# v's loads issued behind their batch's q and k without a gate, one attention session kept in the unturned form, and one output product two slots later

## The chip, the core and the metric

The kernel runs on one core of one Trainium2 chip. The metric is the device time of one launch in microseconds; a lower time is better. The engines are named as in the profile: PE is TensorE (PEld its weight loads), DVE VectorE, ACT ScalarE, POOL GpSimd, SP the sync engine, which here only issues DMAs.

## The reference

```python
def _attn_ref(q, k, v):                     # each 8 x 8 x 576 x 64, float32
    window = 32
    scores = (1 / sqrt(D)) * q @ k^T
    scores = where(abs(pos[:, None] - pos[None, :]) <= window, scores, -1e9)
    attn = exp(scores - max(scores)); attn = attn / (sum(attn) + 1e-9)
    return attn @ v

def _moe_ref(x, w_in, w_out):               # x 4608 x 512, w_in 512 x 2048, w_out 2048 x 512
    h = x @ w_in
    g = where(h >= 1, h, where(h <= -1, 0, (h + 1)**2 / 4))
    return g @ w_out
```

The attention's output, heads side by side, is the x of the second part: batch b's 576 positions are rows 576 b to 576 b + 575.

## The kernel before

**Slots.** The second part is cut into 144 slots of TensorE work, numbered a = 0 to 143. A slot multiplies one piece of `w_in` with 256 or 512 columns of the transposed x (`xT`) into a PSUM buffer `hp` (L664 for 256 columns, L685 for 512; from slot 56 to 135 the wide form). ScalarE makes `rr` from it (L703), then either VectorE makes `mx` and `gT` (L709, L710) or ScalarE makes `mx` (L706) and VectorE `gT` (L707). `hp` has two buffers. The order of all instructions of an engine is the order in which the program writes them; nothing is moved by a scheduler.

**What else a slot holds.** After its `hp` and `rr`, a slot a runs the attention steps that a table gives it (`run(a)`), then the products with `w_out` (`pair`, L636, for the first 512 rows; `unit`, L618 and L609, for the rest), then `run(a + 0.5)`, then the transpositions listed for it. A `pair` makes eight products of 256 columns; four pairs fill one output tile, which ScalarE copies (L641) and SP stores (L642). The list `pairs` gives (slot, pair number); the last tile's four pairs are numbers 14, 12, 15 and 13.

**The attention as a stream.** Batch 0 is treated apart. From batch 1 on, the positions form one stream, cut into turns of two or three 64-position blocks: turns 0 to 4 are batch 1, 5 to 7 batch 2, 8 to 10 batch 3 and so on, three to a batch, up to 22. For a turn k `stream_scores` multiplies q and k (L289), into a PSUM tile `bb` and, for three blocks, the spare halves `sp` of an `hp` and an `op` buffer; ScalarE takes exp (L295, L298) and VectorE applies the mask (L206). `stream_sums` of turn k, in the slot where turn k + 1's scores are made, multiplies with v and divides by the row sums. Turns 4 to 22 have their sums in slots 26, 29, 33, 36, 39, 44, 48, 51, 59, 66, 71, 74, 81, 87, 95, 99, 108, 111 and 123. The sums of turns 8, 11, 14, 17 and 20 are the first to read the v of batches 3 to 7. The sums come in two forms:

- unturned: 32 products with v as the weights and 8 with `ones` as the weights for three blocks (L421; for turns of this form VectorE has added pairs of the masked scores into `rows` at L307 before). The row sums land beside the result and in `sp`; ScalarE takes ln and exp(-ln) of them (L325, L328, L329), VectorE multiplies into `xT` (L333).
- turned (turns in `TURNED`): 48 products with the scores as the weights (L352), v having a column of ones, so that the row sums are a column; VectorE takes a reciprocal (L360) and scales into `xn` (L364), and SP issues three DMA transpositions of `xn` into `xT` (L370, L373).

**The loads.** GpSimd issues all loads from HBM that change the type from float32 to bfloat16: q and k of a batch in two DMAs each (L107), v in four (L117). They go through one software queue in order. q and k of batch b land in one of two buffers by (b + t) mod 2 (t is 0 for q and 1 for k), so that the q of batch b + 1 reuses the k buffer of batch b. From batch 2 on, SP transposes q and k by DMA into `qT` and `kT` (L199), in the slots of `xps`; these, the transpositions of `xn` and all stores of the output share SP's queue in order. v has three buffers, batch b in number b mod 3. v of batches 0 and 1 is loaded at the start. v of batches 2 to 7 is loaded at the end of a transposition's slot, behind a gate: a GpSimd copy of two columns of the transposed tile, which makes GpSimd, and all that it issues later, wait for that transposition:

```python
        for x in xps.get(a, []):
            xpose(*x)
            if x[1] == (x[0] not in EARLY):      # EARLY = 3, 4: behind q's; the others: behind k's
                P.tensor_copy(gate, qkT(*x)[:, 0:2])
                for n in range(4):
                    load_v(x[0], n)
```

The loads of q and k are written at the start of slots 19 and 20 (batch 3), 26 and 27, 37 and 38, 60 and 61, 84 and 85 (batch 7); the transpositions of q and k in slots 7 and 16 (batch 2), 23 and 24, 34 and 35, 49 and 50, 65 and 69, 89 and 91. GpSimd and SP come to their instructions ahead of TensorE where nothing makes them wait.

Of the kernel before, what the change touches and what calls it, by code (L numbers as in the profile page):

```python
# [14 lines left out]
def kernel(  # L15
# [32 lines left out]
    LONG = 2  # L48
    SPLIT = range(20, 25)
    DIRECT = 4, 5  # L50
    EARLY = 3, 4
    TURNED = {6, 9, 10, 12, *range(14, 23)}

    const = ctx.enter_context(tc.tile_pool(name="const", bufs=1))
    nat = ctx.enter_context(tc.tile_pool(name="nat", bufs=2))
# [47 lines left out]
    def load_nat(b, t):  # L103
        src, dst, nm = ((q, qn, "qn"), (k, kn, "kn"))[t]
        x = dst[b] = nat.tile([128, NU, 2, D], BF, name=nm, tag=f"n{(b + t) % 2}", bufs=1)
        for h in range(2):
            nc.gpsimd.dma_start(out=x[:, :, h], in_=src[b, NY * h:NY * h + NY].rearrange("y s d -> (y s) d")  # L107
                                .rearrange("(u p) d -> p u d", p=128))

    def load_v(b, n):  # L110
        if b not in vn:
            vn[b] = vns[b % 3]
            if 2 <= b < 5:
                P.memset(vn[b][:, :, :, D:], 1.0)
        h, a = divmod(n, 2)
        y = NY * h + 2 * a
        nc.gpsimd.dma_start(out=vn[b][64 * a:64 * a + 64, :, h, :D], in_=v[b, y:y + 2].rearrange("y s d -> (y s) d")  # L117
                            .rearrange("(c r) d -> r c d", r=64))
# [48 lines left out]
    def qkT(b, t):  # L167
        if t == 0:
            return qTs[b % 3][:, PAD:]
        if b not in kT:  # L170
            kT[b] = ktp.tile([128, NY * S], BF, name="kT")
        return kT[b]
# [24 lines left out]
    def xpose(b, t):  # L197

        nc.sync.dma_start_transpose(out=qkT(b, t).rearrange("d (u p) -> d u p", p=128),  # L199
                                    in_=(qn, kn)[t][b].rearrange("p u h d -> p (u h d)"))  # L200
# [70 lines left out]
    def stream_scores(k, eng, pool=ps_s):  # L271
# [29 lines left out]
        M = turn_of(k)  # L301
        if k in TURNED or k in DIRECT:
            return
# [9 lines left out]
    def turn_of(k):  # L313

        return next(m for s, e, m in STREAMS if s == turns[k][0])
# [61 lines left out]
    def stream_sums(k, pool=ps_n):  # L377

        if k in TURNED:
            return turned_sums(k, pool)  # L380
# [95 lines left out]
    def flush():  # L476
        while muls:
            muls.pop(0)()
# [20 lines left out]
    def op_tile(shape, nm="op"):  # L499

        turn[0] ^= 1
        return ps_o.tile(shape, FP, name=nm, tag=f"op{turn[0]}")
# [54 lines left out]

    NB = NT // TB
    NF = DFF // 256
    pairs = [(7, 0), (7, 1), (8, 2), (11, 4), (12, 5), (13, 3), (15, 8), (15, 6), (17, 9), (17, 7), (18, 10), (20, 11), (21, 14), (22, 12), (23, 15), (23, 13)]  # L560
    ev = {}

    def at(a, *todo):


        ev.setdefault(a, []).extend(x for x in todo if x)
# [14 lines left out]
    ends_first = [14, 14.5, 15.5, 16, 20, 21.5, 24.5, 27, 28, 34, 37, 38, 40, 42, 45, 46, 49, 50, 52, 54, 55, 57, 58, 62, 63, 67, 68, 69, 73, 76, 77, 78, 80, 84, 86, 88, 90, 91, 93, 94, 96, 97, 98, 101, 103, 104, 106, 110, 112, 114, 117, 120, 121, 122, 127, 130, 132, 134]  # L581
    for n, a in enumerate(sl):
        at(a, seq[first_sl + n][0], seq[first_sl + 1 + n][1] if first_sl + 1 + n < len(seq) else (stream_sums, len(seq), ps_s))
    loads, xps = {}, {}
    for t, a in enumerate([7, 16]):
        xps.setdefault(a, []).append((2, t))
    for b in range(LONG + 1, B):
        a = [19, 26, 37, 60, 84][b - 3]
# [7 lines left out]
    def home(t):  # L596

        return (3 - t % 4 if t % 4 in (0, 3) else t % 4) if WIDE[0] <= NF * t < WIDE[1] else t % 4
# [29 lines left out]
    def pair(x):  # L628

        half, p, g = x // 8, x % 8 // 4, x % 4  # L630
        if (half, p) not in op:
            op[half, p] = op_tile([128, 2, 256]), []
        o, done = op[half, p]
        for tt in range(2):
            for j in range(4 * g, 4 * g + 4):
                nc.tensor.matmul(o[:, tt], gT[:, j, p, 128 * tt:128 * tt + 128], w_out[:, j, 256 * half:256 * half + 256],  # L636
                                 start=not done, stop=len(done) == 4 * NF - 1, skip_group_check=True)
                done.append(j)
        if len(done) == 4 * NF:
            osb = osp.tile([128, DM], FP, name="osb")  # L640
            A.copy(osb, o.rearrange("p t f -> p (t f)"))  # L641
            nc.sync.dma_start(out=out[256 * p:256 * p + 256, 256 * half:256 * half + 256]  # L642
                              .rearrange("(t p) f -> p t f", p=128), in_=osb.rearrange("p (t f) -> p t f", t=2))

    def run(pos):
        todo = []
        spares.clear()
        for fn, *x in ev.get(pos, []):
            if fn in (sums, stream_sums):
                todo.append(fn(*x))  # L650
                if pos in ends_first:
                    todo.pop()()
            elif fn is tposes:
                tposes(*x)
            else:
                pool = (x.pop(),) if x[-1] in (ps_s, ps_n, ps_o) else ()
                fn(*x, None if pos < bias_until else V, *pool)
        for end in todo:
            end()

    def project(hp, f, r0, todo, first, last):

        for n, (j, kk) in enumerate(todo):
            nc.tensor.matmul(hp[:, j], w_in[:, kk, 256 * f + 128 * j:256 * f + 128 * j + 128],  # L664
                             xT[:, kk, r0:r0 + TB], start=first and n == 0, stop=last and n == len(todo) - 1,
                             skip_group_check=True)
# [5 lines left out]
    for a in range(NF * NB + 2 * NF):  # L672
        wide = WIDE[0] <= a < WIDE[1]
        for b, x in loads.get(a, []):
            load_nat(b, x)
        if a == 0 or a > 3:
            flush()
        if a < NF * NB:
            if wide:
                n, f = divmod(a - WIDE[0], 2 * NF)  # L680
                t = WIDE[0] // NF + 2 * n
                r0 = TB * t % RING
                hp = ps_h.tile([128, 2, TB], FP, name="hp", tag="hp")
                for n, kk in enumerate((0, 2, 1, 3)):
                    nc.tensor.matmul(hp.rearrange("p n t -> p (n t)"), w_in[:, kk, 128 * f:128 * f + 128],  # L685
                                     xT[:, kk, r0:r0 + 2 * TB], start=n == 0, stop=n == 3)
                g = gT[:, f, home(t):home(t + 1) + 1:home(t + 1) - home(t)]
            else:
                t, f = order[a] if a < len(order) else divmod(a, NF)
                r0 = TB * t % RING  # L690
                if a in (0,):
                    hps = [ps_h.tile([128, 2, TB], FP, name="hp", tag="hp") for _ in range(2)]
                    for y in range(2):
                        for n in range(2):
                            project(hps[n], f + n, r0, [(j, y + 2 * m) for j in range(2) for m in range(2)], y == 0, y == 1)
                elif not hps:
                    hps = [op_tile([128, 2, TB], "hp") if a in [6] else ps_h.tile([128, 2, TB], FP, name="hp", tag="hp")]
                    project(hps[0], f, r0, [(j, kk) for j in range(2) for kk in (0, 2, 1, 3)], True, True)
                hp = hps.pop(0)
                g = gT[:, 2 * f:2 * f + 2, home(t)]  # L700

            rr = ewp.tile([128, 2, TB], FP, name="rr")
            A.activation(rr, hp, AF.Relu, scale=0.5, bias=0.5)  # L703
            mx = ewp.tile([128, 2, TB], FP, name="mx")
            if a in two_on_act:
                A.activation(mx, rr, AF.Square)  # L706
                V.scalar_tensor_tensor(g, hp, 1.0, mx, op0=ALU.max, op1=ALU.min)  # L707
            else:
                V.tensor_max(mx, hp, rr)  # L709
                V.scalar_tensor_tensor(g, rr, 1.0, mx, op0=ALU.min, op1=ALU.mult)  # L710
        flush()
        run(a)
        for n, x in pairs:
            if n == a:
                pair(x)
        for x in range(done, done + units[a]):
            unit(x)
        done += units[a]
        run(a + 0.5)
        for x in xps.get(a, []):  # L720
            xpose(*x)
            if x[1] == (x[0] not in EARLY):
                P.tensor_copy(gate, qkT(*x)[:, 0:2])  # L723
                for n in range(4):
                    load_v(x[0], n)


# [28 lines left out]
```

## Time and profile before

| | |
|---|---|
| time, median of 3 runs | 303.62 us (303.17 to 303.64) |
| profiled execution | 305.74 us, of it the span of the program's instructions 303.9 us |
| granted TensorE clock, mean over the span | 0.994 |
| busy: TensorE | 289.2 us (95%) |
| busy: VectorE, ScalarE, GpSimd | 227.0, 184.3 and 79.5 us |
| software queue, hardware queue | 18.06 MB and 19.38 MB, packet time 92.4% and 32.4% of 16 DMA engines' span |

A row of a timeline reads: start in us, duration in us (of a merged run of instructions, first start to last end), engine, line, operation, output<-inputs, form, count, and in brackets the idle time of the engine before it and what ended that. "SPq" rows are SP's issuing of a DMA, not its transfer. A row for one tile gives the least, median and greatest duration in ns, the first and last start, and the line under it the time from issue to landing.

### The profile page before, as it was taken

The numbers are of one execution on the slowest core, as the hardware profiler recorded it, in microseconds if no ns is written. First come the engines' busy times: TensorE is split into PE (matmuls) and PEld (weight loads), VectorE is DVE, ScalarE is ACT, GpSimd is POOL, SyncE is SP. The second block draws the span as 40 slices with busy tenths as digits, with TensorE's granted clock in tenths as the row PEclk, the third lists the DMA queues.
The fourth block names the chain that finished last, engine by engine and source line by source line (L and its number), as shares of the span: only waits on it lengthen the run. The fifth ranks groups of instructions, "written<-read, shape, count | busy, mean of one in ns | idle before, by whom it ended". The sixth has DMA issues, their size and how long they took to land.

```text
span 303.9 us, 8062 instructions
## 1 busy us (share of the span) xinstructions
PE 289.2 (95%) x3345; PEld 171.4 (56%) x3376; DVE 227.0 (75%) x370; ACT 184.3 (61%) x331; POOL 79.5 (26%) x101
## 2 busy tenths in 40 slices
PE   8789999999999997999999999999999999999995
PEld 3467878877666665654444444444444444446644
DVE  5278888978987988599888898597878887546700
ACT  4687794777677663655765566565566435785301
POOL 8795730073091083009105500013000000000000
PEclk9999999999999999799999999999999999999999
DMA  9999999999999999999999993399312211100021
GB/s 152 182 180 200 187 178 152 213 130 145 173 152 142 159 183 131 164 232 109 155 192 111 168 157 55 78 176 111 90 37 63 60 37 56 42 35 36 37 104 69
DMA packets 149204, 38.24 MB, mean 126 GB/s; under 512 B 133552, under 2 KB 145584, under 8 KB 149168
## 3 DMA queue, kind: packets, MB, share of 16 engines
q0 software_dynamic: 103056, 18.06, 92.4%
q1 hardware_dynamic: 45968, 19.38, 32.4%
q8 instruction: 26, 0.43, 0.6%
q10 hardware_dynamic: 144, 0.29, 0.4%
q14 instruction: 10, 0.08, 0.1%
HBM read 36.70 MB, written 9.44 MB: 152 GB/s over the span
## 4 chain that ended last, share of the span: by engine, by line
PE 77%; DMA 12%; POOL 5%; issue 3%; ACT 3%; DVE 0%; POOLq 0%; ACTq 0%
PE op L618 31%; PE hp L685 23%; PE hp L664 12%; DMA vn<-in_v_dram 6%; DMA w_in<-in_moe_w_in_dram 4%; PE op L636 4%; POOL vn L117 2%; POOL w_in L122 2%; PE bb L352 2%; DMA qT<-qn 2%; PE bb L289 1%; PE op L609 1%; PE bb L421 1%; PE tp L192 1%; ACT rr L703 1%
## 5 line engine op out<-in xcount | busy, mean ns | idle before, releaser
L703 ACT ACTIVATE rr<-hp 128x512 f32<-128x512 f32 x144 | 85.5, 595 | 86.1 <-PE hp L685 47.6
L618 PE MATMUL op<-w_out,gT 128*128 128x512 bf16 x472 | 121.2, 381 | 3.2 <-issue 3.0
L709 DVE TENSOR_TENSOR mx<-hp,rr 128x512 f32<-128x512 f32 x104 | 71.3, 685 | 19.2 <-ACT rr L703 18.4
L685 PE MATMUL hp<-xT,w_in 128*128 128x512 bf16 x315 | 80.7, 379 | 0.3
L618 PEld LDWEIGHTS <-gT 128*128 128x128 bf16 x496 | 47.1, 98 | 50.3 <-issue 0.6
L710 DVE SCALAR_TENSOR_TENSOR gT<-rr,mx 128x512 bf16<-128x512 f32 x104 | 72.2, 694 | 3.6
L664 PE MATMUL hp<-xT,w_in 128*128 128x256 bf16 x512 | 66.7, 275 | 2.1 <-DMA w_in<-in_moe_w_in_dram 1.4
L664 PEld LDWEIGHTS <-w_in 128*128 128x128 bf16 x512 | 49.3, 98 | 17.5 <-issue 2.4
L685 PEld LDWEIGHTS <-w_in 128*128 128x128 bf16 x320 | 31.2, 98 | 37.9 <-issue 0.3
L707 DVE SCALAR_TENSOR_TENSOR gT<-hp,mx 128x512 bf16<-128x512 f32 x40 | 27.5, 688 | 18.4 <-ACT mx L706 16.3
L117 POOL DMA_DIRECT2D vn<-in_v_dram x32 | 27.3, 871 | 4.9 <-issue 1.5
L295 ACT ACTIVATE wt<-bb 128x1024 bf16<-128x1024 f32 (+2 forms) x23 | 22.1, 966 | 6.6 <-PE bb L289 5.1
L706 ACT ACTIVATE mx<-rr 128x512 f32<-128x512 f32 x40 | 25.2, 630 | 1.3
L723 POOL COPY gate<-kT 128x2 bf16<-128x2 bf16 x4 | 1.3, 325 | 90.4 <-DMA kT<-kn 90.4
L206 DVE TENSOR_TENSOR wt<-wt,mask 128x1408 bf16<-128x1408 bf16 (+4 forms) x23 | 19.5, 847 | 7.0 <-ACT wt L298 5.7
L622 ACT COPY osb<-op 128x512 f32<-128x512 f32 x23 | 13.3, 578 | 10.9 <-PE op L618 10.9
L636 PE MATMUL op<-w_out,gT 128*128 128x256 bf16 x128 | 16.0, 273 | 0.4 <-ACT rc L325 0.4
L107 POOL DMA_DIRECT2D qn<-in_q_dram x12 | 14.8, 1252 | 2.6 <-DMA kn<-in_k_dram 1.9
L107 POOL DMA_DIRECT2D kn<-in_k_dram x12 | 14.8, 1261 | 0.9 <-DMA vn<-in_v_dram 0.8
L636 PEld LDWEIGHTS <-gT 128*128 128x128 bf16 x128 | 12.4, 98 | 2.2 <-DMA w_out<-in_moe_w_out_dram 0.7
L364 DVE TENSOR_TENSOR xn<-bb,rs 128x512 bf16<-128x512 f32 (+1 forms) x26 | 13.3, 552 | 0.4
L298 ACT ACTIVATE wt<-sp 128x256 bf16<-128x256 f32 (+1 forms) x36 | 11.1, 367 | 0.0
(89 smaller groups left out, 185.2 us busy)
## 6 DMA issues: line engine op xcount, KB each, us to landing
out_dram<-osb SPq DMA_DIRECT2D x30, 256.0 KB, 2.7
vn<-in_v_dram POOLq DMA_DIRECT2D x32, 144.0 KB, 6.5
qn<-in_q_dram POOLq DMA_DIRECT2D x12, 288.0 KB, 10.1
kn<-in_k_dram POOLq DMA_DIRECT2D x12, 288.0 KB, 12.8
out_dram<-osb SPq DMA_DIRECT2D x12, 128.0 KB, 1.9
w_in<-in_moe_w_in_dram POOLq DMA_DIRECT2D x11, 128.0 KB, 4.9
w_out<-in_moe_w_out_dram POOLq DMA_DIRECT2D x4, 256.0 KB, 8.9
w_out<-in_moe_w_out_dram POOLq DMA_DIRECT2D x2, 512.0 KB, 13.6
```

Of the source, the lines that this page charges most:

```text
L107: nc.gpsimd.dma_start(out=x[:, :, h], in_=src[b, NY * h:NY * h + NY].rearrange("y s d -> (y s) d") .rearrange("(u p) d -> p u d", p=128))
L117: nc.gpsimd.dma_start(out=vn[b][64 * a:64 * a + 64, :, h, :D], in_=v[b, y:y + 2].rearrange("y s d -> (y s) d") .rearrange("(c r) d -> r c ...
L295: A.activation(wt[:, :, w0 + lo:w0 + cut], ps.rearrange("p h (y j) -> p (h y) j", y=2)[:, :, lo:cut], AF.Exp, scale=D ** -0.5)
L618: nc.tensor.matmul(op[tt], gT[:, j, home(tt // 2), 128 * (tt % 2):128 * (tt % 2) + 128], w_out[:, j], start=j == 0, stop=j == 15)
L636: nc.tensor.matmul(o[:, tt], gT[:, j, p, 128 * tt:128 * tt + 128], w_out[:, j, 256 * half:256 * half + 256], start=not done, stop=len(done ...
L664: nc.tensor.matmul(hp[:, j], w_in[:, kk, 256 * f + 128 * j:256 * f + 128 * j + 128], xT[:, kk, r0:r0 + TB], start=first and n == 0, stop=l ...
L685: nc.tensor.matmul(hp.rearrange("p n t -> p (n t)"), w_in[:, kk, 128 * f:128 * f + 128], xT[:, kk, r0:r0 + 2 * TB], start=n == 0, stop=n == 3)
L703: A.activation(rr, hp, AF.Relu, scale=0.5, bias=0.5)
L706: A.activation(mx, rr, AF.Square)
L707: V.scalar_tensor_tensor(g, hp, 1.0, mx, op0=ALU.max, op1=ALU.min)
L709: V.tensor_max(mx, hp, rr)
L710: V.scalar_tensor_tensor(g, rr, 1.0, mx, op0=ALU.min, op1=ALU.mult)
```

## The change

Three edits. The gates of batches 3 to 7 go: their v is loaded at the start of slots 20, 27, 40, 61 and 85, directly behind the same batch's q and k for batches 3, 4, 6 and 7, and two slots behind them for batch 5. Batch 2 keeps a gate, at the transposition of its q (slot 7) instead of its k (slot 16). Turn 6, whose sums stand in slot 33, leaves `TURNED` and takes the unturned form; its scores, in slot 29, get the addition into `rows`. Pair 13 moves from slot 23 to slot 25, and with it the copy and the store of that output tile.

```diff
-    EARLY = 3, 4
-    TURNED = {6, 9, 10, 12, *range(14, 23)}
+    TURNED = {9, 10, 12, *range(14, 23)}
...
-    pairs = [(7, 0), (7, 1), (8, 2), (11, 4), (12, 5), (13, 3), (15, 8), (15, 6), (17, 9), (17, 7), (18, 10), (20, 11), (21, 14), (22, 12), (23, 15), (23, 13)]
+    pairs = [(7, 0), (7, 1), (8, 2), (11, 4), (12, 5), (13, 3), (15, 8), (15, 6), (17, 9), (17, 7), (18, 10), (20, 11), (21, 14), (22, 12), (23, 15), (25, 13)]
...
+    vslots = [20, 27, 40, 61, 85]
...
         for b, x in loads.get(a, []):
             load_nat(b, x)
+        if a in vslots:
+            for n in range(4):
+                load_v(LONG + 1 + vslots.index(a), n)
...
             xpose(*x)
-            if x[1] == (x[0] not in EARLY):
+            if x == (LONG, 0):
                 P.tensor_copy(gate, qkT(*x)[:, 0:2])
                 for n in range(4):
-                    load_v(x[0], n)
+                    load_v(LONG, n)
```

## The prediction

> **What bounds the kernel now.** I read the page first (busy time, the slices, the chain that ended last), then the waits, then the timelines around each wait. The three lines are the engines' busy time, the DMA slices and the chain by engine.
>
> ```profile
> PE 289.2 (95%) x3345; PEld 171.4 (56%) x3376; DVE 227.0 (75%) x370; ACT 184.3 (61%) x331; POOL 79.5 (26%) x101
> ...
> DMA  9999999999999999999999993399312211100021
> ...
> PE 77%; DMA 12%; POOL 5%; issue 3%; ACT 3%; DVE 0%; POOLq 0%; ACTq 0%
> ```
>
> TensorE is busy 95% of the span and carries 77% of the chain, so time is won only where TensorE stands still or runs slowly. But the DMA engines are at 90% or more through the first 24 slices, some 182 us: a second resource lies close behind. Two lines of the waits, "waiting line <- releaser: us in total, times, longest", and three of TensorE's timeline show what v does:
>
> ```profile
> POOL gate L723 <- DMA kT<-kn: 90.4, 4, 32.3
> ...
> PE bb L421 <- DMA vn<-in_v_dram: 2.0, 4, 0.8
> ```
>
> ```profile
> 94.00 0.45 PE L421 MATMUL bb<-wt,vn 64*64 64x96 bf16 x24 [0.33 <-DMA vn<-in_v_dram]
> ...
> 119.00 0.23 PE L421 MATMUL bb<-wt,vn 64*64 64x96 bf16 x2 [0.78 <-DMA vn<-in_v_dram]
> 119.97 0.45 PE L421 MATMUL bb<-wt,vn 64*64 64x96 bf16 x24 [0.74 <-DMA vn<-in_v_dram]
> ```
>
> GpSimd stands 90.4 us at the gate, and the v loads queued behind it reach TensorE late: for batch 3 at 94.0 (0.33 us) and for batch 4 at 119 (0.78 + 0.74). That is 1.85 us of TensorE; the rest of the 2.0 is batch 1, which the change does not touch. The stall at 119 has a second price, seen when the span is cut at the clock's own edges (PE and PEld busy, then DVE, ACT, POOL, and PEclk):
>
> ```profile
> 117.95:121.36 3.41, 1.74 (x67) 1.30 (x68) 2.28 (x4) 1.08 (x2) 0.00 (x0) 1.00 1.67 156
> 121.36:124.77 3.41, 3.41 (x14) 1.76 (x13) 1.54 (x3) 3.25 (x8) 0.00 (x0) 0.50 2.03 151
> ```
>
> After 3.41 us in which TensorE was busy 1.74, the granted clock was 0.50 for the next 3.41 us: half of 3.41, 1.71 us of matmul work, is lost. The Trainium skill ("TensorE: Matmul & The Clock Gate", Part 1) ties the half clock to a whole idle window of about 3.4 us that runs freely. The trace agrees on the length and not on the depth: the window before was only half idle. By the page's rule this dip would not belong to the stall and would stay.
>
> **The v loads, part by part.** Today each batch's q and k loads, their transpositions on SP's queue, and only then (behind the gate) v, follow one another. GpSimd's timeline:
>
> ```profile
> 62.45 0.68 POOL L723 COPY gate<-kT 128x2 bf16<-128x2 bf16 x1 [20.77 <-DMA kT<-kn]
> ...
> 66.53 2.47 POOL L107 DMA_DIRECT2D qn<-in_q_dram  x2
> ...
> 82.76 0.32 POOL L723 COPY gate<-qT 128x2 bf16<-128x2 bf16 x1 [11.35 <-DMA qT<-qn]
> ...
> 87.38 2.45 POOL L107 DMA_DIRECT2D qn<-in_q_dram  x2 [0.52 <-DMA kT<-kn]
> ```
>
> Five gates go; batch 2's stays but waits for q's transposition instead of k's. The next rows are one tile's DMAs each: count, ns of issue, first and last start, and below it the time from issue to landing. They give the prices of the transfers.
>
> ```profile
> L199 SPq DMA_TRANSPOSE qT<-qn x1: 3807/3807/3807, 51.4 to 51.4; - x1
> DMA to landing us min/median/max: 5.8/5.8/5.8
> ...
> L117 POOL DMA_DIRECT2D vn<-in_v_dram x4: 852/859/885, 63.2 to 65.7; - x4
> DMA to landing us min/median/max: 4.9/5.1/5.7
> ...
> L107 POOL DMA_DIRECT2D kn<-in_k_dram x2: 1267/1271/1275, 68.9 to 70.1; - x2
> DMA to landing us min/median/max: 9.6/9.8/10.0
> ...
> L199 SPq DMA_TRANSPOSE kT<-kn x1: 2857/2857/2857, 80.4 to 80.4; - x1
> DMA to landing us min/median/max: 6.4/6.4/6.4
> ```
>
> v of batch 2: four issues 0.85 us apart; the second lands at 64.0 + 4.9 = 68.9 and the fourth at 65.7 + 5.7 = 71.4, so 1.25 us each, 5.0 for the four, and 71.4 - 63.2 = 8.2 from first issue to end. The q and k loads behind it end at 70.1 + 10.0 = 80.1: 8.7 us. k's transposition ends at 80.4 + 6.4 = 86.8, which is 6.7 after the last k load. Now the new order. Batch 2's q is transposed at 51.4 + 5.8 = 57.2; the gate opens 5.2 us earlier than 62.45, v is issued at about 57.9 and ends at 57.9 + 8.2 = 66.1. The q of batch 3 need not wait for v's 3.4 us of issues any more, only for batch 2's k transposition (62.4, since the buffer is shared): 62.6 instead of 66.5. Its q and k end at 66.1 + 8.7 = 74.8, its v at 74.8 + 5.0 = 79.8, and TensorE asks at 94.0. Batch 4's q is issued about 0.6 behind batch 3's k transposition, near 87; 8.7 + 5.0 + some 2 to 3 us of start give v by 104, asked at 119. Both stalls go: -1.85 us, and with the second the half clock, -1.71, where an execution has it. Batches 5 to 7 have no v stall now and get v earlier still.
>
> What is late next? Transfers of the software queue hold a transposition back, which the gate had kept away from v:
>
> ```profile
> L107 POOL DMA_DIRECT2D kn<-in_k_dram x2: 1237/1242/1247, 89.8 to 91.0; - x2
> DMA to landing us min/median/max: 12.5/12.6/12.8
> ...
> L199 SPq DMA_TRANSPOSE qT<-qn x1: 5282/5282/5282, 98.5 to 98.5; - x1
> DMA to landing us min/median/max: 8.9/8.9/8.9
> ```
>
> This one took 8.9 us against 5.8 above, since k's loads ended only at 91.0 + 12.8 = 103.8, and it landed 3.6 behind them. The Trainium skill ("DMA: Bandwidth & Descriptors", Queues, rings and completion order) says that a DMA engine takes turns between its queues packet by packet. By that rule a transposition would share from the start and batch 3's k would be ready well before 86; the trace shows it finishing behind the loads, so I sum with it queued behind v. Then batch 3's k transposition ends at 79.8 + 6.7 = 86.5, and its scores are asked for here:
>
> ```profile
> 87.03 0.37 PE L289 MATMUL bb<-qT,kT 64*64 64x96 bf16 x16
> ```
>
> Today 86.8 against 87.0, afterwards 86.5: the same knife-edge, cover 0.5 us. I take a cost of 0; the bounds are an end 2 us earlier (no cost) and one 2 us later (batch 2's k transposition slowed by v beside it), which stalls 1.5 us.
>
> **The session behind slot 33.** The rows of the turned session (slot 33) and of the unturned one of the same form in slot 36:
>
> ```profile
> 82.96 0.60 ACT L703 ACTIVATE rr<-hp 128x512 f32<-128x512 f32 x1 [0.85 <-ACT wt L298]
> ...
> 88.79 0.41 ACT L325 ACTIVATE rc<-bb 128x256 f32<-128x256 f32 x1
> 89.06 0.69 ACT L328 ACTIVATE rc<-sp 128x256 f32<-128x256 f32 x2
> 89.78 0.84 ACT L329 ACTIVATE rc<-rc 128x768 f32<-128x768 f32 x1
> ```
>
> ```profile
> 82.93 1.04 PE L664 MATMUL hp<-xT,w_in 128*128 128x256 bf16 x8
> ```
>
> ```profile
> 83.80 1.02 DVE L364 TENSOR_TENSOR xn<-bb,rs 128x512 bf16<-128x512 f32 x2
> ...
> 89.88 0.56 DVE L307 TENSOR_TENSOR rows<-wt 128x768 bf16<-128x768 bf16 x1
> 90.66 0.96 DVE L333 TENSOR_TENSOR xT<-bb,rc 128x768 bf16<-128x768 f32 x1 [0.22 <-ACT rc L329]
> ```
>
> ScalarE gains 0.41 + 0.69 + 0.84 = 1.94 us between L298 and the next rr; 0.85 of it was idle there, so rr of slot 34 comes some 1.1 us later. VectorE adds 0.56 (earlier, at slot 29, where it idles) and trades 1.02 for 0.96. On TensorE 48 products become 40; three transpositions leave SP's queue. On the path: the hp buffer's spare half is now read until L328 ends. ScalarE's idle began at 82.96 - 0.85 = 82.11; L325 and L328 take 89.78 - 88.79 = 0.99, so the buffer is free at 83.1 and a signal later, where hp of slot 35 started at 82.93: about +0.35. The ones products wait for the same buffer ahead of the next scores: about +0.2. I take +0.55, an estimate; bounds 0 (ScalarE's idle before the next slots hides it) and 1.1 (rr's whole delay).
>
> **The product from slot 23 to 25.** Eight products move behind hp of slot 25. TensorE's two waits there:
>
> ```profile
> 65.03 1.03 PE L664 MATMUL hp<-xT,w_in 128*128 128x256 bf16 x8 [0.22 <-DVE mx L709]
> ...
> 66.94 0.31 PE L289 MATMUL sp<-qT,kT 64*64 64x128 bf16 x8 [0.25 <-DVE gT L707]
> ```
>
> The product now fills the first, and hp of slots 24 and 25 come earlier, so VectorE clears the second: -0.47, bounds -0.47 and 0. Its store moves in SP's queue behind batch 3's two transpositions; the output buffer is asked for again only three copies later, so 0.
>
> **Given back.** -1.85 - 1.71 - 0.47 + 0.55 = -3.48 with the half clock, -1.77 without. The loads' cadence (q, k, v, then transpositions that free the buffers) keeps its length per batch, so TensorE runs into it. The tightest place later is slot 88, whose xT comes by SP:
>
> ```profile
> 187.87 1.03 PE L685 MATMUL hp<-xT,w_in 128*128 128x512 bf16 x4
> ```
>
> ```profile
> L373 SPq DMA_TRANSPOSE xT<-xn x2: 1186/1206/1226, 180.9 to 182.1; - x2
> ...
> DMA to landing us min/median/max: 4.5/5.6/6.6
> ```
>
> They land by 182.1 + 4.5 = 186.6; the last is needed by the third matmul, half of 1.03 after 187.87, so slack is about 1.7 us. If batch 7's loads end no earlier, 3.48 would be cut to 1.7; if the transpositions move up with TensorE, nothing is cut. I take 1.0 back with the half clock and 0.15 without: -2.5 and -1.6. The middle is -2.1.
>
> **The sum.** The profiled execution took 305.74 us (span 303.9, 1.8 around it): 303.6 after. The median of the runs is 303.62, 2.1 less than the profiled one; the half clock's 1.71 may be missing in them, which is why I take the middle. 303.62 - 2.1 = 301.5. A measurement of this kernel can tell about 0.2%, 0.6 us, from no change.
>
> **Rivals.**
> *Slower: v holds k's transposition past its scores.* The place is slot 36, asked at 87.0. For it: batch 3's transposition meets its scores within 0.2 us now, and there v's 5.0 us is queued ahead. Against it: the loads start 3.9 us earlier. It decides when it ends 2 us late, near 89: that stall halves a window like the one at 118 and brings its own half clock, 2 + 1.71 = 3.7 against the gain of 2.1: 305.2. With all of v's 5.0 added to today's 86.8 the stall is 4.8: 308. The page's rule of taking turns speaks against this one. Chance 0.26.
> *Most of it is given back.* The waits vanish, no execution without the profiler had the half clock, slot 33 costs its 1.1, the product wins nothing and slot 88 takes 0.15: -1.85 + 1.1 + 0.15 = -0.6: 303.0 and up. Chance 0.14.
> *Nothing is given back.* The half clock was in every run and slot 88's transpositions move up: -3.48: 300.1. Chance 0.15.
> *The change does not do what it says*: if v were queued behind the next batch's q, it would come no earlier. The order of GpSimd's instructions excludes it: v of batch 3 stands directly behind its k.
>
> **How the numbers follow.** The forecast has 0.45, with 0.15 for the larger gain faster by over 0.2% is 0.60; within 0.2% is 0.14; slower 0.26. Low end 300.0, the larger gain; the high end 304.9 reaches into the slower rival, up to a stall just under 2 us, leaving out about 0.2.
>
> **What would show it.** Right: no L421 wait on vn at 94 and 119, v of batch 4 landed near 104, PEclk without a dip near 121, hp of slot 26 without its 0.22, three SP transpositions fewer. Wrong: L289 waiting on kT near 87 (the slower rival), a wait of L685 on xT at slot 56 or 88 (given back), a half clock at a new place, or the L421 waits still there.

## The result, and the profile after

The changed kernel takes 306.09 us, the kernel before 303.53 us (medians of 16 executions each, on the same chip), 2.6 us or 0.8% more. As a ratio with its 95% interval it is 1.010 (1.0072 to 1.0128). That is above the forecast's range and within the 305.2 to 308 of the slower rival. All ratios leave out executions that took over 1.5% more than the fastest of their kernel, two of twelve in e3 and three of twelve in e5 among them.

The profiled execution after took 306.88 us (span 305.1, mean granted clock 0.994), against 305.74 before (303.9, 0.994). The page of the changed kernel, its busy times, DMA slices and chain by engine:

```profile
PE 289.3 (95%) x3337; PEld 171.9 (56%) x3368; DVE 227.3 (75%) x369; ACT 186.1 (61%) x335; POOL 78.0 (26%) x96
...
DMA  9999999999999999999999999592212201100121
...
PE 83%; DMA 8%; POOL 4%; issue 2%; ACT 2%; DVE 2%; POOLq 0%; ACTq 0%; DVEq 0%
```

TensorE did the same work, 289.3 us against 289.2, in a longer span. The DMA engines are at 90% or more through the first 25 slices instead of 24. The waits of the changed kernel (line, releaser: us, times, longest) hold one that was not there:

```profile
PE bb L288 <- DMA kT<-kn: 3.2, 1, 3.2
...
POOL qn L106 <- DMA kT<-kn: 75.1, 5, 21.0
```

The waits on v in slots 39 and 51 are gone, as the edit meant, and so is the gate's 90.4 us (at batch 2's gate 16.0 us are left); GpSimd now waits in front of q's loads. In their place TensorE waits 3.2 us for batch 3's transposed k. Its timeline at slot 36:

```profile
86.50 0.54 PE L420 MATMUL bb<-wt,vn 64*64 64x64 bf16 x32
86.93 0.28 PE L420 MATMUL sp<-rows,ones 64*64 64x256 bf16 x4
90.41 0.39 PE L288 MATMUL bb<-qT,kT 64*64 64x96 bf16 x16 [3.19 <-DMA kT<-kn]
```

TensorE asks for the scores at 87.2, within 0.2 us of where the prediction put it, and gets k at 90.4. The half clock came back with this stall. Three windows of 3.41 us around it (PE and PEld busy, then DVE, ACT, POOL, and the granted clock):

```profile
84.99:88.40 3.41, 2.22 (x52) 1.37 (x49) 2.76 (x5) 1.45 (x3) 0.00 (x0) 1.00 1.33 207
88.40:91.81 3.41, 1.25 (x28) 0.84 (x30) 0.26 (x1) 0.96 (x2) 0.88 (x1) 1.00 0.54 202
91.81:95.22 3.41, 3.41 (x15) 1.97 (x14) 2.41 (x3) 2.56 (x7) 3.41 (x4) 0.50 1.29 83
```

The second window was busy for 1.25 us, and the third ran at 0.50. So in the profiled executions one stall and its half clock took the place of the other: -1.85 of v and +3.19 of k make +1.34, and the two half clocks cancel. The executions differ by 1.14.

Why k came late is read from the rows of single tiles in the changed kernel (issue in ns, first and last start, and below it the time from issue to landing). They are, in this order, v of batch 2, k of batch 3, v of batch 3, and the transpositions of batch 3's q and k:

```profile
L116 POOL DMA_DIRECT2D vn<-in_v_dram x4: 855/862/885, 58.2 to 60.7; - x4
DMA to landing us min/median/max: 6.8/8.2/9.0
...
L106 POOL DMA_DIRECT2D kn<-in_k_dram x2: 1227/1232/1237, 66.7 to 67.9; - x2
DMA to landing us min/median/max: 10.1/10.3/10.5
...
L116 POOL DMA_DIRECT2D vn<-in_v_dram x4: 890/898/909, 69.2 to 71.7; - x4
DMA to landing us min/median/max: 10.0/13.2/14.9
...
L198 SPq DMA_TRANSPOSE qT<-qn x1: 7251/7251/7251, 74.0 to 74.0; - x1
DMA to landing us min/median/max: 12.8/12.8/12.8
...
L198 SPq DMA_TRANSPOSE kT<-kn x1: 5372/5372/5372, 81.4 to 81.4; - x1
DMA to landing us min/median/max: 8.9/8.9/8.9
```

v of batch 2 ends at 60.7 + 9.0 = 69.7, batch 3's k at 67.9 + 10.5 = 78.4. v of batch 3 lands from 69.2 + 10.0 = 79.2 to 71.7 + 14.9 = 86.6, and q's transposition beside it takes 12.8 us, where the same one took 5.7 in the profile before (76.6 to 82.3). k's transposition stands behind q's on SP's queue and lands at 81.4 + 8.9 = 90.3: 12.0 us behind the last k load.

### The profile page after: what moved, and what is told of

Read it like the earlier page. It is cut to its first block, busy times and chain, and to the rows that moved or that the text cites. A ratio compares the mean times of both kernels' runs of the same rounds, so it can differ in the third digit from the quotient of the medians.

```text
span 305.1 us, 8036 instructions
## 1 busy us (share of the span) xinstructions
PE 289.3 (95%) x3337; PEld 171.9 (56%) x3368; DVE 227.3 (75%) x369; ACT 186.1 (61%) x335; POOL 78.0 (26%) x96
## 4 chain that ended last, share of the span: by engine, by line
PE 83%; DMA 8%; POOL 4%; issue 2%; ACT 2%; DVE 2%; POOLq 0%; ACTq 0%; DVEq 0%
PE op L618 34%; PE hp L688 23%; PE hp L664 15%; DMA w_in<-in_moe_w_in_dram 5%; PE op L636 4%; DMA kT<-kn 3%; PE bb L351 2%; POOL w_in L121 2%; PE bb L288 1%; PE bb L420 1%; PE op L609 1%; POOL vn L116 1%; PE tp L191 1%; ACT rr L706 1%; ACT wt L294 1%
## 5 line engine op out<-in xcount | busy, mean ns | idle before, releaser
L106 POOL DMA_DIRECT2D qn<-in_q_dram x12 | 14.6, 1223 | 77.5 <-DMA kT<-kn 75.1
L363 DVE TENSOR_TENSOR xn<-bb,rs 128x512 bf16<-128x512 f32 (+1 forms) x24 | 12.2, 551 | 0.4
L288 PE MATMUL bb<-qT,kT 64*64 64x128 bf16 (+1 forms) x360 | 8.7, 215 | 3.2 <-DMA kT<-kn 3.2
L332 DVE TENSOR_TENSOR xT<-bb,rc 128x768 bf16<-128x768 f32 (+4 forms) x13 | 9.1, 708 | 3.0 <-ACT rc L328 3.0
## 6 DMA issues: line engine op xcount, KB each, us to landing
kn<-in_k_dram POOLq DMA_DIRECT2D x12, 288.0 KB, 10.5
```

## The experiments

Each kernel is timed against the kernel before on its own chip. The edits are shown against the changed kernel unless said otherwise; "kT lag" is the time in the profiled execution from the landing of batch 3's last k load to that of its transposed k (6.7 in the first profile before).

| label | what is in it | ratio to before, 95% | kT lag, us |
|---|---|---|---|
| e1_v_only | the v loads' edit alone | 1.0143 (1.0096 to 1.0190) | 11.3 |
| e2_rest_only | the two other edits alone | 1.0051 (1.0021 to 1.0081) | 5.5 |
| e3_gate_v3 | the change, batch 3's v behind q's transposition | 0.9973 (0.9942 to 1.0003) | 5.4 |
| e5_half_v3 | the change, two of batch 3's four v loads so | 1.0050 (1.0013 to 1.0086) | 7.2 |
| e9_gate_v7 | the change, batch 7's v gated | 1.0095 (1.0061 to 1.0129) | 9.7 |
| e6_gate_v3_v7 | both gated | 1.0019 (0.9988 to 1.0050) | 5.4 |
| e7_e6_turned | e6, turn 6 turned | 1.0075 (1.0040 to 1.0110) | 5.4 |
| e8_e6_pair23 | e6, pair 13 in slot 23 | 1.0000 (0.9972 to 1.0028) | 5.3 |
| e10_v6_behind_k7 | e6, batch 6's v behind batch 7's k | 1.0006 (0.9973 to 1.0039) | 5.4 |
| e11_v4_only | of batches 3 to 7, only batch 4's v ungated | 0.9988 (0.9963 to 1.0013) | 5.6 |
| e12_change_again | the change | 1.0120 (1.0079 to 1.0161) | 9.7 |
| e13_before_again | the kernel before | 1.0006 (0.9976 to 1.0035) | 5.4 |

### Which of the edits costs

The first two kernels take the change apart. e1 goes back in the turned session and the pair; e2 has only these two:

```diff
 # e1
-    TURNED = {9, 10, 12, *range(14, 23)}
+    TURNED = {6, 9, 10, 12, *range(14, 23)}
-    ... (23, 15), (25, 13)]
+    ... (23, 15), (23, 13)]
 # e2, against the kernel before
-    TURNED = {6, 9, 10, 12, *range(14, 23)}
+    TURNED = {9, 10, 12, *range(14, 23)}
-    ... (23, 15), (23, 13)]
+    ... (23, 15), (25, 13)]
```

> The kernel before with the v edit alone (turn 6 stays turned, pair 13 stays in slot 23). Theory T: batch 3's v, queued ahead of batch 3's transpositions, makes the k transposition land some 3 us after slot 36 asks for it (3.2 us of stall) and brings a half clock (1.7 us), while the v waits at slots 39 and 51 go. By T nearly all of the change's effect is in this edit: some 306, 0.7 to 1.2% above the kernel before, a wait of L289-like products on kT of 2.5 to 4 us near 90, no wait on vn at 94 and 119. Rival U: the unturned session and the moved product cost the time; then this kernel is level with the kernel before or below it (301 to 303.5).

> The kernel before with the other two edits alone (turn 6 unturned, pair 13 in slot 25), v gated as before. T: within 0.2% of the kernel before (the prediction's +0.55 and -0.47), the vn waits at 94 and 119 still there, hp of slot 26 without its 0.22 us wait. U: 1% slower, about 306.

e1 is slower by 1.43%, some 4.3 us: the v loads' edit carries the whole loss, and in its trace TensorE waits 2.17 us at 89.2 for the same transposed k, at a granted clock of 1.000: without a half clock. e2 is slower too, by 0.51%, and its profiled execution has a wait that the change doesn't have. TensorE's timeline of e2 at slot 29:

```profile
72.21 0.41 PE L421 MATMUL bb<-wt,vn 64*64 64x96 bf16 x20 [1.20 <-DMA vn<-in_v_dram]
```

There v of batch 2 still stands behind k's transposition and lands at 72.17, and TensorE comes for it 1.2 us too early. The two parts are not additive: 1.43 and 0.51 against 1.00 for both.

### Is it batch 3's v in front of batch 3's transpositions

e3 leaves everything of the change but one thing: batch 3's four v loads wait for the transposition of batch 3's q. e5 lets two of the four go ahead:

```diff
 # e3
-    vslots = [20, 27, 40, 61, 85]
+    vslots = [27, 40, 61, 85]
-                load_v(LONG + 1 + vslots.index(a), n)
+                load_v(LONG + 2 + vslots.index(a), n)
-            if x == (LONG, 0):
+            if x in ((LONG, 0), (3, 0)):
-                    load_v(LONG, n)
+                    load_v(x[0], n)
 # e5
-            for n in range(4):
+            for n in range(2 if a == 20 else 4):
                 load_v(LONG + 1 + vslots.index(a), n)
-            if x == (LONG, 0):
-                for n in range(4):
-                    load_v(LONG, n)
+            if x in ((LONG, 0), (3, 0)):
+                for n in range(0 if x[0] == LONG else 2, 4):
+                    load_v(x[0], n)
```

> The changed kernel, with batch 3's v alone put back behind the gate at its q's transposition; batches 4 to 7 stay ungated and batch 2 keeps the gate at q. T: batch 3's k transposition lands by 87, no stall at slot 36 and no half clock there, the waits at 119 stay away: 4 to 5 us below the changed kernel, 301 to 302, about 0.6% faster than the kernel before; a wait on vn of up to 0.4 us may come back near 94. Rival W: it is batch 2's earlier v that slows batch 2's k transposition and so all of batch 3; then the stall near 87 to 90 stays (over 1.5 us) and the time is 304 to 306.

> The changed kernel with two of batch 3's four v loads ungated in slot 20 and two behind the gate at its q's transposition: half the dose. T, with the transposition queued behind the loads: the k transposition lands about 1.5 to 2 us earlier than in the changed kernel (near 88 to 88.5), the stall is 1 to 1.8 us, and the half clock may or may not come: 302.5 to 305. W: no difference from the changed kernel (306).

e3 takes the loss away: 0.9973 against 1.0100, 1.3% or 3.9 us for four loads in one place. e5 stands between, at 1.0050. The last k load and k's transposition, first of e3, then of e5 (an execution of 310.06 us, read for its landings and waits and not for its time):

```profile
L106 POOL DMA_DIRECT2D kn<-in_k_dram x2: 1229/1233/1237, 64.9 to 66.1; - x2
DMA to landing us min/median/max: 8.8/8.9/9.0
...
L198 SPq DMA_TRANSPOSE kT<-kn x1: 3295/3295/3295, 75.3 to 75.3; - x1
DMA to landing us min/median/max: 5.2/5.2/5.2
```

```profile
L106 POOL DMA_DIRECT2D kn<-in_k_dram x2: 1229/1233/1237, 65.4 to 66.6; - x2
DMA to landing us min/median/max: 9.2/9.6/10.0
...
L198 SPq DMA_TRANSPOSE kT<-kn x1: 3982/3982/3982, 77.9 to 77.9; - x1
DMA to landing us min/median/max: 5.9/5.9/5.9
```

k landed at 75.1 and 76.6, its transposed tile at 80.5 and 83.8: lags of 5.4 and 7.2 us for no v load and two between, where four gave 9.7 to 12.0. That is a dose with three steps, and time follows it (e5's interval still overlaps the change's). It shows the cause: the v loads queued between k and its transposition. Through which wait they cost time it does not show: in e5's trace the transposed k landed 2.0 us ahead of its scores (85.8), and TensorE lost 3.47 us in front of slot 88 instead.

Two rows of e3's trace show what came next: TensorE's at slot 88, and the transpositions that it waits for.

```profile
184.86 1.44 PE L688 MATMUL hp<-xT,w_in 128*128 128x512 bf16 x3 [2.56 <-DMA xT<-xn]
```

```profile
L372 SPq DMA_TRANSPOSE xT<-xn x2: 1248/1292/1337, 175.2 to 176.6; - x2
DMA to landing us min/median/max: 9.2/9.8/10.8
```

That is the place which the prediction named for gains given back. A stall of 2.56 us there brought a half clock of its own in this execution (304.3 us, mean clock 0.994). Two more of e3's twelve had 0.994 (305.4 and 310.1 us); the nine others were granted 0.998 or more and have a mean of 301.3 us.

### Slot 88

e6 gates batch 7's v as well, behind k's transposition; e9 gates batch 7's alone and leaves batch 3's where the change has it. e10 also puts batch 6's v behind batch 7's q and k:

```diff
 # e6, against e3
-    vslots = [27, 40, 61, 85]
+    vslots = [27, 40, 61]
-            if x in ((LONG, 0), (3, 0)):
+            if x in ((LONG, 0), (3, 0), (7, 1)):
 # e9
-    vslots = [20, 27, 40, 61, 85]
+    vslots = [20, 27, 40, 61]
-            if x == (LONG, 0):
+            if x in ((LONG, 0), (7, 1)):
-                    load_v(LONG, n)
+                    load_v(x[0], n)
 # e10, against e6
-    vslots = [27, 40, 61]
+    vslots = [27, 40, 85]
```

> The changed kernel with v of batches 3 and 7 gated as before (at q's and at k's transposition), 4 to 6 ungated, 2 gated at q. Theory T: the queue order is the whole matter, and the second place where v stands ahead of a transposition that TensorE needs is batch 7's v ahead of the xT transpositions for slot 88 (2.56 us of wait on xT there with batch 3's v gated alone). So the wait at slot 88 goes or falls under 0.5 us, the last of the three transpositions lands 3 to 5 us earlier after its issue, and the time falls by another 1 to 2.5 us: 299 to 300.5, 0.7 to 1.2% below the kernel before. Rival X: slot 88 is held by the q and k loads of batch 7 and not by v; then the wait stays near 2.5 us and the time near 301.5.

> The changed kernel with batch 7's v alone gated as before; batch 3's stays ahead of its transpositions. T: the stall at slot 36 and its half clock stay, and as TensorE then comes late to slot 88, gating batch 7's v wins nothing: level with the changed kernel, 305 to 306.5, 1% above the kernel before. If instead slot 88 is part of the loss of the changed kernel, it is 1 to 2 us faster than that: 304 to 305.

> The changed kernel with v of batch 3 gated at q's transposition, v of batch 7 gated at k's, and v of batch 6 moved from slot 61 to slot 85, behind batch 7's q and k; v of batches 4 and 5 ungated. Rival X of the run before held: with batch 7's v gated the transpositions for slot 88 still land late (184 to 187), behind batch 7's q and k loads, which start only when batch 6's k transposition, itself queued behind batch 6's v, has freed the buffer. By that, batch 6's k transposition lands 5 us earlier (157 to 160), batch 7's q and k land by 172 to 175, the transpositions for slot 88 land by 181, and no wait is left there: 299.5 to 301.5, 0.5 to 1% below the kernel before. If instead the DMA engines' total work sets slot 88, the landing stays at 184 or later and the time at 302 to 302.7.

e9 is level with the change (1.0095 and 1.0100): batch 7's v costs nothing there. e6 and e9 ran side by side on one chip and differ in batch 3's v alone: 1.0019 against 1.0095, the same cause a second time, at 0.8%, and somewhat smaller than between e3 and the change. In e6 TensorE waited 0.47 us in front of slot 88, and its xT tiles still landed at 183.6 to 184.0, which leaves batch 7's q and k loads to hold them. e10 moves those forward: batch 7's last k load landed at 175.3 instead of e3's 182.2. Slot 88's transpositions in its trace:

```profile
L372 SPq DMA_TRANSPOSE xT<-xn x2: 1185/1206/1226, 176.2 to 177.4; - x2
DMA to landing us min/median/max: 5.0/5.1/5.8
```

They take 5.1 us instead of 9.8 and land by 182.5 instead of 185.8, and nothing waits for them. The time stays level with before (1.0006). The mechanism is there, but it was worth nothing that these runs can tell. The traces show a pattern all the same: of the nine with v of batch 6 loaded in slot 61, all but the changed kernel's own wait 0.4 to 3.5 us in front of slot 88; of the five in which that v is gated or moved (before, e2, e10, e11 and e13), none does.

### The session and the product

e7 is e6 with turn 6 turned again, e8 is e6 with pair 13 in slot 23:

```diff
 # e7, against e6
-    TURNED = {9, 10, 12, *range(14, 23)}
+    TURNED = {6, 9, 10, 12, *range(14, 23)}
 # e8, against e6
-    ... (23, 15), (25, 13)]
+    ... (23, 15), (23, 13)]
```

> The kernel with batches 3 and 7 gated, and turn 6 turned again as in the kernel before. T, with the prediction's +0.55 for the unturned form: 0.3 to 1 us faster than the unturned one. Rival U: its three transpositions on SP's queue hold batch 4's q transposition or land late for slot 40, and it is 0.5 to 2 us slower, with a wait on xT or kT between 95 and 115.

> The kernel with batches 3 and 7 gated, and pair 13 back in slot 23. By the prediction's -0.47 for the move it is 0.47 us slower (0.15%), the 0.22 and 0.25 us waits at slot 26 back; if the move is worth nothing, level within 0.1%.

With the session turned e6 loses 0.56%, 1.7 us: the unturned form is a gain here. The waits of e7, then batch 4's q loads and SP's issue of their transposition, in e7 and then in e6, show a way for part of it:

```profile
PE hp L688 <- DVE wt L205: 1.6, 1, 1.6
PE bb L288 <- DMA kT<-kn: 1.3, 1, 1.3
```

```profile
L106 POOL DMA_DIRECT2D qn<-in_q_dram x2: 1274/1276/1277, 83.5 to 84.7; - x2
DMA to landing us min/median/max: 9.5/10.1/10.7
...
95.62 6.60 SPq L198 DMA_TRANSPOSE qT<-qn  x1
```

```profile
L106 POOL DMA_DIRECT2D qn<-in_q_dram x2: 1274/1276/1277, 83.8 to 85.0; - x2
DMA to landing us min/median/max: 9.3/9.4/9.5
...
94.62 6.65 SPq L198 DMA_TRANSPOSE qT<-qn  x1
```

SP does not stand behind the turned session's three transpositions: it has issued them, and a store, by 88.5, and then waits for batch 4's q. But they are in flight until 94.2, beside the q loads, which are issued 0.3 us earlier in e7 and land 1.0 us later (95.5 against 94.5). So q's transposition starts 1.0 us later, and batch 4's transposed k lands at 111.45 instead of 109.9, where e7 waits 1.33 us. The 1.6 us are in front of slot 88, at 186.0; its xT tiles landed at 185.9 to 186.4, so this is a late transposition too, whatever engine the line names. e8 is level with before and with e6: the two small waits of slot 26 (0.22 and 0.25) are back in its trace, and the time doesn't show them.

### Was there anything to gain

Of the gates of batches 3 to 7, e11 removes only the one that the forecast's larger part hung on, batch 4's, which holds back the v of slot 51 (its other edits are the change's); e12 and e13 are the two kernels once more, without an edit:

```diff
 # e11
-    vslots = [20, 27, 40, 61, 85]
+    vslots = [27]
-                load_v(LONG + 1 + vslots.index(a), n)
+                load_v(LONG + 2 + vslots.index(a), n)
-            if x == (LONG, 0):
+            if x in ((LONG, 0), (3, 0), (5, 1), (6, 1), (7, 1)):
-                    load_v(LONG, n)
+                    load_v(x[0], n)
```

> The changed kernel with v of batches 3, 5, 6 and 7 gated as before, so that only batch 4's v (and batch 2's gate at q) is earlier. If the waits at slots 39 and 51 were worth their 1.85 us alone, it is 0.5 to 2 us below the kernel before, 300.5 to 302; the last transposition for slot 88 lands before 185. If the kernel before ordinarily has slack that swallows these waits, it is level, 302.5.

> The changed kernel once more, on the chip of the two runs above, so that they stand beside it directly: 305.5 to 306.5, 1% above the kernel before, with a granted clock of 0.994 in more than half of its executions and near 1.000 in those of the kernel before.

> The kernel before, unchanged, for a second profiled execution of it. In the first the half clock cost 1.7 us and v kept TensorE waiting 1.85 us, and it was 2.1 us above the median of the runs. Theory Y: these waits belong to that execution more than to the kernel; then this one has a granted clock of 0.998 or more, L421 waits on vn of less than 1 us in all between 60 and 125, and a span of 301 to 302.5. If the waits are the kernel's own, the 0.78 and 0.74 us at 119 are back within 0.5 us in sum, and the gain from getting v of batch 4 earlier was swallowed elsewhere.

e11 gains nothing that can be told (0.9988); its trace has no wait at slot 51, but 0.51 us on v at 92.9 and 1.51 us on a transposed k at 112.2. e13's profiled execution shows a reason. Its v loads of batches 3 and 4, and TensorE's rows in slots 39 and 51:

```profile
L117 POOL DMA_DIRECT2D vn<-in_v_dram x4: 857/873/886, 81.9 to 84.4; - x4
DMA to landing us min/median/max: 4.8/5.0/6.5
...
L117 POOL DMA_DIRECT2D vn<-in_v_dram x4: 857/872/886, 103.7 to 106.2; - x4
DMA to landing us min/median/max: 5.7/6.1/7.7
```

```profile
93.69 0.52 PE L421 MATMUL bb<-wt,vn 64*64 64x32 bf16 x32
...
117.70 0.52 PE L421 MATMUL bb<-wt,vn 64*64 64x32 bf16 x32
...
119.44 0.24 PE L289 MATMUL bb<-qT,kT 64*64 64x128 bf16 x2 [0.83 <-issue]
```

v lands by 84.4 + 6.5 = 90.9 and 106.2 + 7.7 = 113.9, 2.8 and 3.8 us ahead of its use. There is no wait on v and no half clock: the span is 301.1 us, the clock 1.000. (In the last row TensorE has stood 0.83 us, for which the profile names no cause.) So the stalls on which the forecast rested are not in every execution of this kernel. The granted clock of all executions says more. One half window costs 1.71 of some 305 us, which makes a mean clock of 0.994. Of 97 executions of the kernel before, timed beside the experiments, 94 had 0.998 or more. For the 16 beside the changed kernel no clock is on record but the profiled one's; their median, 303.5, lies 1.0 to 1.8 us above the medians of the 97 (301.8 to 302.6), so the stalls may have been more frequent there. Of the changed kernel's 16, eleven had 0.994 or less, with a mean of 306.7 us against 305.1 for the other five. With batch 3's v ahead of its transpositions (the change, e1, e9, e12) it is 25 of 37 executions; with that v gated and the session unturned (e3, e6, e8, e10, e11) 4 of 60; e5, with half of it gated, has 3 of 12, and e7, with the session turned, 5 of 12. The half clock is thus part of the loss, and the five executions at 305.1 show that it is not all of it.

The changed kernel's own stall varies as well. e12's profiled execution, TensorE at slot 36:

```profile
87.65 0.39 PE L288 MATMUL bb<-qT,kT 64*64 64x96 bf16 x16 [0.56 <-DMA kT<-kn]
```

Here it was 0.56 us with a span of 301.9, while the median of e12 was 305.2: a profile of this kernel that alone would have shown the change as harmless. In e9's profiled execution k met its scores with no wait at all, at a clock of 1.000, and yet it took 305.0 us, e9's median. Its span is 3.2 us longer than e6's (303.2 and 300.0): by the starts of the slots, 1.3 of it arose before slot 8, where TensorE waits 1.2 us for weights, and 1.5 at slot 88, where it waits 1.94 us for xT. So not every slow execution is slow by the stall at slot 36.

## Why the prediction was wrong

**The step that failed** is the price of batch 3's k transposition, taken as 0 with a bound of 2 us late. Three of its numbers held. v of batch 2 was issued at 58.2 (57.9 forecast); the q and k loads ended 78.4 - 69.7 = 8.7 behind it (8.7); and k's transposition landed 12.0 behind k (5.0 + 6.7 = 11.7). The last held by luck: v ended 86.6 - 78.4 = 8.2 behind k and not 5.0, k's transposition 90.3 - 86.6 = 3.7 behind v and not 6.7, and in e9 and e12 the lag was 9.7. What failed is the end of batch 2's v: 8.2 us after its first issue by a row in which the queue ahead was empty, 11.5 in the changed kernel, where batch 2's k transposition was still under way (56.6 + 7.0 = 63.6) and none of the v had landed (58.2 + 6.8 = 65.0). In the eleven traces with this early v it took 10.3 to 12.0 us, in the three with it behind k's transposition 8.2 to 9.6. So everything behind it slid by 3.6 us on to a place where the prediction itself had counted 0.5 us of cover. This account is read from rows: no run puts batch 2's v alone back, and e3, which keeps it early, has no loss, so by itself it costs nothing that can be told. Nor did it bring the loads forward as the prediction counted: in e13, with that v behind the gate, batch 3's k landed at 77.1, in the change's two traces at 78.4 and 77.9. The prediction did name the mechanism, in the bound and in the slower rival; it took the price from the row without a neighbour.

**The slower rival** described what happened in the profiled execution: k's transposition held past slot 36 by v queued ahead, with a half clock behind it, 305.2 to 308. Measured are 306.1 in the median, and 3.19 us of wait with the half clock in the profile. Other executions came to their loss otherwise (e1's stall without a half clock, e9's without the stall).

**The rule that was weighed.** The Trainium skill ("DMA: Bandwidth & Descriptors", Queues, rings and completion order) has a DMA engine take turns between its queues packet by packet. This trace agrees that they share: v's four loads land 2.5 us apart ((86.6 - 79.2) / 3) instead of 1.25, and q's transposition beside them takes 12.8 us instead of 5.7. What the prediction drew from the rule, k ready well before 86, doesn't follow, and the trace contradicts it: as the rows read, two transpositions share with v one behind the other, and k's is the second. The sum with k's transposition queued behind v, which the prediction used, gave this execution's lag within 0.3 us, with both of its parts off by 3 us in opposite directions.

**The v waits, -1.85, and the half clock, -1.71.** Both went from the profile, as forecast (no wait on vn at slots 39 and 51, though v of batch 4 landed at 98.4 + 12.2 = 110.6 rather than near 104). They were worth nothing that these runs can tell: e13's execution has neither, and e11, which of batches 3 to 7 ungates only batch 4's v, is level. The prediction counted the waits in full and the half clock by half, though the median lay 2.1 us below the profiled execution; that difference was the warning that the waits too might belong to the execution.

**The unturned session, +0.55.** The sign was wrong. hp of slot 35 starts at 82.94, as before (82.93), so the buffer's cost did not appear; what the sum set at nothing, three transpositions fewer beside the loads, is a gain in e7 against e6 (1.7 us; each of the two ratios is known to 0.3 or 0.35%). In e2's one profile, without the v edit, the earlier TensorE runs into another wait; whether that is e2's loss is not shown.

**The pair, -0.47.** The two waits vanish and return as forecast, but e8 gives no time for it: 1.0000 against 1.0019.

**Given back at slot 88.** The changed kernel hardly reached this (0 and 0.43 us there in its two profiles); in the first, slot 36 had taken the time already. Where TensorE was early, in e3's profile, it did: 2.56 us, from the loads of batch 7 as the prediction said. e10 frees it without a measurable gain.

What stays open: why one execution has 3.19 us at slot 36, another 0.56 and e9's none, and by which waits batch 3's v costs time in the executions without the half clock. In the two profiles of the change k landed at 78.4 and 77.9, and the lag was 12.0 and 9.7 us; what makes the lag vary was not tried.

## What to carry to other kernels

Before a stall in a profile is counted as a gain, set the profiled execution beside the median: if it is longer by about the stall, as 305.74 against 303.6 was here, the stall may be its own; a second profile and the granted clocks of all executions tell more. Price a transfer from a row that has the neighbours it will have after the change, not from the row with an empty queue. Where a tile is due within half a microsecond of its use, as here, nothing should be queued between its load and the transposition that it needs; what is due later goes behind it.

## What the runs showed of the hardware

Loads of the software queue and transpositions of SP's queue slow each other down: 0, 2 and 4 v loads between k and its transposition made that land 5.4, 7.2 and 9.7 to 12.0 us behind k, and the four v loads of batch 2 took 10.3 to 12.0 us where they were issued while a k transposition was under way, 8.2 to 9.6 behind it. The half clock again followed a window that was only partly idle, 1.25 us busy of 3.41 with 0.50 granted in the next. The Trainium skill ("TensorE: Matmul & The Clock Gate", Part 1) asks for a whole idle window; both dips seen here, after 1.74 and 1.25 us of work, speak against that depth, while a window with 2.22 us of work was followed by a full clock.
